# Decay attention and a soft mixture of experts on one core: the opening in another order with fewer filling products, part of the second layer in 256 columns, three more homes for expert weights

## The chip, the core and the metric

The kernel runs on one core of a Trainium2 chip. The time is device microseconds of the whole execution, and a kernel's time is the median of its runs. TensorE does the matrix products (PE; PEld is its weight load), VectorE (DVE), ScalarE (ACT) and GpSimd (POOL) do the rest, and SyncE (SP) issues every DMA of this kernel.

## What is computed

Two stages. The first is attention over 64 heads (8 batches of 8 heads), 576 tokens of width 64, with a causal mask and a decay that is a running sum of log f:

```python
log_f = np.log(np.clip(f, 0.0001, 1.0))
cum = np.cumsum(log_f, axis=-1)
decay = cum[:, :, :, None] - cum[:, :, None, :]
scores = np.where(causal, -1000000000.0, scale * q @ k.T + decay)
attn = np.exp(scores - np.max(scores, axis=-1, keepdims=True))
attn_out = (attn / (np.sum(attn, axis=-1, keepdims=True) + 1e-09)) @ v
```

The second takes its output as x (4608 tokens, width 512) through 32 slots of 8 experts, four slots each; softmax over all tokens on the way in (d), over slots on the way out (c):

```python
logits = x @ phi
slot_input = d.T @ x
for e in range(E):
    slot_out[e] = np.maximum(slot_input[e] @ w1[e], 0.0) @ w2[e]
out = c @ slot_out
```

Everything is float32. The weights w1 and w2 are 32 MB, the output 9.4 MB.

## The kernel before

**Attention.** The 64 heads are worked as 32 pairs, head i = 2g or 2g+1. Every product of 32-bit numbers q and k is made of rounded parts (WA for k, YA for q, rounded by ACT in `round_k` and `round_q`) and remainders (WB, YB; the remainders are subtracted on POOL by `low_k` and `low_q`, the rounded halves are copied beside them by a DMA, `dup_k` and `dup_q`). For a head PE makes scores with queries on the partitions (`s1`, L224), DVE takes their row maxima (`tops`, L240 and L238), PE turns the maxima (`mturn`, L250), ACT copies them (`mrows`, L259) and a DMA puts them as one more row into YA; then PE makes the scores again with keys on the partitions and the maxima already inside (`s2`, L277 and L278), ACT takes the exponential into PTS (`expo`, L284), POOL blanks what lies above the diagonal (`causal`, L292 for three blocks and L295 for the last two), and PE multiplies by V (`s3`, L312, 25 products a head), after which DVE divides (`norm`). A head's maxima are made one pair ahead of its `s2`. Scores of `s1` go to three PSUM tiles in rotation, those of `s2` to the three tiles of `ring`.

**Opening.** The first heads are written out by hand, call by call, ahead of the loop: `first(i, n)` is a quarter of `s1` and `tops` of head i, `both(i, n)` a quarter of `s2` and `expo`, `warm(n, cs)` n products whose result nobody reads (L495, "filling products"). Pair 0 gets its maxima by two transposes a head (`first_rows`, L573 and L576). Each engine runs its own instructions in the order in which the calls stand, and so does SP's DMA queue.

**The loop** over pairs g = 1 to 31 interleaves `s2` of pair g with `s1` of the pair after, turns pair g-1 of x (`px`, L339, copied by `xcopy`), and takes along the first steps of the mixture for a finished batch b (logits, a running maximum and sum, the slot inputs in `dispatch`, token weights in `combine`).

**Expert weights** are 64 quarters of 512 KB, used in the order `ORDER`. 27 have tiles of their own and are loaded in the loop; the others get a home as something else is finished with (`wstream`): buffers of q and k, of PTS, V and x, pools that open where the attention's tiles close, and, from the 45th on, the tiles of quarters that are used up.

**After the loop** the last batch's logits, sum and slot inputs run as one chain with other work between (`dispatch(b - 1, ...)`, `cols`). Then come the experts: `mlp1` (L910) makes four products of 256 columns for each quarter, each into another 32 partitions; `mlp2` (L948) makes for experts 0 to 3 two products of 512 columns a quarter, the first quarter of a half step into partitions 0 to 31 and 32 to 63, the second into the other 64, and for experts 4 to 7 four of 256. The output products (`blocks`, L1021) begin between the last of them; ACT and DVE copy them and SP writes them out.

## Time and profile before

| | us |
|---|---|
| median of three runs | 393.11 (392.79 to 394.31) |
| the profiled execution | 394.05 |
| its span, first to last instruction | 392.4 |
| PE, DVE, ACT, POOL busy | 372.9, 280.7, 260.1, 252.6 |
| mean granted clock of PE | 0.987 |

The span is 1.65 us shorter than the profiled execution's own time. Busy times are sums over a whole span that has four stages with different limits: opening (to 27 us), loop (to 324), the chain and the experts (to 362), output (to the end).

### The profile page before, as it was taken

Reading aid. Unit: us, or ns where it says so; the run is one execution under the profiler, and the core shown is the slowest. Engines: PE = TensorE matmul, PEld = TensorE weight load, DVE = VectorE, ACT = ScalarE, POOL = GpSimd, SP = SyncE. Lnnn points to the kernel's source line nnn. Section 1 sums busy time; section 2 is a strip of 40 time slices with the busy share of each in tenths; the row PEclk is TensorE's granted clock in tenths of the full one; section 3 lists DMA queues with packets and bytes.
Section 4 is the critical chain, followed back from the end, with each engine's and each line's share of the span. In section 5 each row is a group of like instructions: output and inputs, shape, how many; then the busy total and the mean of one; then the engine's idle time right before and its main releaser. Section 6 shows DMA issues by size and latency. Waiting matters only on the chain.

```text
span 392.4 us, 15020 instructions
## 1 busy us (share of the span) xinstructions
PE 372.9 (95%) x5827; PEld 330.1 (84%) x5827; DVE 280.7 (72%) x1074; ACT 260.1 (66%) x664; POOL 252.6 (64%) x349
## 2 busy tenths in 40 slices
PE   7999999999999999999999999999999999999860
PEld 7889999999999999999999999999899986545630
DVE  7878887878787878787879787878687535441761
ACT  8859786868686778677877686868686652021650
POOL 4797887878787878787878787878687831100000
PEclk9999999999999999999999999999999999999995
DMA  6865768677867777768777778778775879999798
GB/s 205 212 160 162 217 167 273 194 217 206 251 192 211 218 225 211 214 186 241 210 214 207 217 218 260 212 211 252 225 210 155 256 282 319 408 408 358 258 383 327
DMA packets 34343, 93.71 MB, mean 239 GB/s; under 512 B 4266, under 2 KB 8288, under 8 KB 34272
## 3 DMA queue, kind: packets, MB, share of 16 engines
q1 hardware_dynamic: 34272, 92.75, 76.3%
q8 instruction: 46, 0.75, 0.8%
q14 instruction: 25, 0.20, 0.2%
HBM read 63.93 MB, written 9.73 MB: 188 GB/s over the span
## 4 chain that ended last, share of the span: by engine, by line
PE 88%; DMA 4%; DVE 3%; ACT 2%; issue 1%; SPq 0%; ACTq 0%; DVEq 0%
PE pv L312 25%; PE ring L277 14%; PE s L224 13%; PE ring L278 13%; PE pv L339 5%; PE pv L948 4%; PE more L910 4%; PE lg L375 3%; DMA out<-RAW 2%; PE ds L459 2%; PE ring L495 1%; DMA YA<-mr 1%; PE pv L250 1%; DMA PTS<-in_f 1%; ACT PTS L284 1%
## 5 line engine op out<-in xcount | busy, mean ns | idle before, releaser
L284 ACT ACTIVATE PTS<-ring 128x320 f32<-128x320 f32 (+2 forms) x256 | 119.8, 513 | 65.2 <-PE ring L278 36.2
L277 PE MATMUL ring<-YA,WA 67*128 67x320 f32 (+9 forms) x384 | 121.9, 330 | 0.1
L240 DVE CUSTOM_DVE_ANT_0 s<-s,mask 128x320 f32<-128x320 f32 (+3 forms) x256 | 109.1, 442 | 5.4 <-PE s L224 0.9
L278 PE MATMUL ring<-YB,WB 128*128 128x320 f32 (+4 forms) x384 | 110.7, 296 | 0.0
L312 PE MATMUL pv<-V,PTS 128*64 128x65 f32 x3200 | 104.5, 223 | 1.1 <-ACT mr L259 0.7
L312 PEld LDWEIGHTS pv<-V,PTS 128*64 128x64 f32 x3200 | 99.7, 137 | 4.0 <-issue 1.8
L224 PE MATMUL s<-WA,YA 66*128 66x288 f32 (+9 forms) x384 | 98.5, 312 | 0.5 <-ACT YA L182 0.2
L203 POOL TENSOR_TENSOR WB<-RAW,WB 64x576 fp32r<-64x576 f32 x64 | 90.3, 1411 | 11.6 <-DMA WB<-WA 5.6
L208 POOL TENSOR_TENSOR YB<-RAW,YA 64x576 fp32r<-64x576 f32 x64 | 89.5, 1416 | 2.5
L277 PEld LDWEIGHTS ring<-YA,WA 67*128 67x128 f32 (+3 forms) x384 | 69.7, 183 | 5.8 <-issue 2.1
L278 PEld LDWEIGHTS ring<-YB,WB 128*128 128x128 f32 (+1 forms) x384 | 69.9, 182 | 0.0
L224 PEld LDWEIGHTS s<-WA,YA 66*128 66x128 f32 (+1 forms) x384 | 62.9, 190 | 7.0 <-ACT PTS L284 1.3
L295 POOL TENSOR_SCALAR_AFFINE_SELECT PTS<-PTS 128x128 f32<-128x128 f32 (+1 forms) x128 | 31.5, 268 | 25.6 <-ACT PTS L284 23.8
L240 DVE DVE_READ_ACCUMULATOR2_ANT MT<- 128x1 f32 x310 | 44.0, 142 | 0.0
L292 POOL TENSOR_SCALAR_AFFINE_SELECT PTS<-PTS 128x384 f32<-128x384 f32 x64 | 33.4, 522 | 15.1 <-ACT PTS L284 11.1
L339 PE MATMUL pv<-cs,X 128*128 128x128 f32 x155 | 42.0, 276 | 0.2 <-DVE lg L817 0.2
L240 DVE CUSTOM_DVE_ANT_0 s<-s,mask,MT 128x288 f32<-128x288 f32 x62 | 32.6, 526 | 11.4 <-PE s L224 2.4
L177 ACT CAST WA<-RAW 64x576 fp32r<-64x576 f32 x64 | 40.1, 669 | 0.8
L182 ACT CAST YA<-RAW 64x576 fp32r<-64x576 f32 x63 | 39.5, 669 | 0.4
L327 DVE TENSOR_SCALAR rl<-pv 128x5 f32<-128x5 f32 x64 | 10.5, 164 | 36.6 <-PE pv L312 36.0
L332 DVE TENSOR_TENSOR X<-pv,rl 128x320 f32<-128x320 f32 (+1 forms) x65 | 31.5, 486 | 2.4 <-DVE rl L328 0.3
L363 ACT COPY XT<-pv 128x128 f32<-128x128 f32 (+1 forms) x124 | 28.5, 290 | 0.0
(212 smaller groups left out, 373.1 us busy)
## 6 DMA issues: line engine op xcount, KB each, us to landing
w<-in_w SPq DMA_DIRECT2D x47, 512.0 KB
RAW<-in_qk SPq DMA_DIRECT2D x31, 576.0 KB
V<-in_v SPq DMA_DIRECT2D x32, 325.0 KB
...
```

What stands on the lines that cost most here:

```text
L177: nc.scalar.copy(WA[g % 3][0:64, S * h : S * h + S], RAW[g % 3][64:128, h])
L182: nc.scalar.copy(YA[g % 3][0:64, h, 64:640], RAW[g % 3][0:64, h])
L203: nc.gpsimd.tensor_tensor(t[0:64], RAW[g % 3][64:128, h], t[64:128].bitcast(F32), op=ALU.subtract)
L208: nc.gpsimd.tensor_tensor(YB[g % 2][64:128, h], RAW[g % 3][0:64, h], YA[g % 3][0:64, h, 64:640].bitcast(F32), op=ALU.subtract)
L224: nc.tensor.matmul(t[:, o : o + w], ya[0:m, h, 128 * blk : 128 * blk + 128], wa[0:m, j0 : j0 + w], start=True, stop=True)
L240: nc.vector.tensor_tensor_reduce(out=t[:, o : o + w], in0=t[:, o : o + w], in1=mask[:, m0 : m0 + w], scale=1.0, scalar=top if n == 3 else ...
L277: nc.tensor.matmul(o, wa[0:m, j0 : j0 + n], ya[0:m, h, 64 + i0 : 64 + i0 + w], start=True, stop=False)
L278: nc.tensor.matmul(o, wb[:, j0 : j0 + n], yb[:, h, i0 : i0 + w], start=False, stop=True)
L284: nc.scalar.activation(PT[i % 2][:, SEG_O[bank] : SEG_O[bank] + at], t[:, 0:at], AF.Exp, scale=0.125)
L292: nc.gpsimd.affine_select(d3, d3, pattern=[[0, 3], [1, 128]], compare_op=ALU.is_ge, fill=0.0, base=0, channel_multiplier=-1)
L312: nc.tensor.matmul(o[64 * u : 64 * u + 64, t, :], PT[i % 2][:, at : at + 64], V[:, g % 2, c, 65 * h : 65 * h + 65], start=(c == 0), stop=( ...
L339: nc.tensor.transpose(pm[:, 0:128], x[:, t, 128 * (p % 2) : 128 * (p % 2) + 128], ident)
```

## The change

1. *Opening.* RAW1's load moves behind the first `dup_k`; the second `dup_k`, the second `dup_q` and V's first load come earlier in SP's queue, the constant rows of tiles 2 and pair 2's load later. `fill` lies in X2, so that V's load need not wait for it. Of the filling products behind the first eleven, 15 become 9. `causal(0)` is cut in two, `low_k(2)` and `low_q(2)` stand earlier, `low_k(3)` and `low_q(3)` before `causal(1)`. `both(1, 2)`, `first(3, 2)` and `first(3, 3)` stand before `s3(0)`, `first(4, 1)` before `s3(1)`.
2. *Loop.* One quarter's load a pair for g = 2 to 28, in place of g = 4 to 28 with two at 22 and 26. In the last pair `px(30, 0)` stands after a block of `s2`; in the last two `mturn` and `mrows` stand before an `expo`. In pair 31 half of the last batch's logits stand between `s3(62)` and `s3(63)`.
3. *Homes.* XT's four tiles are one tile XTS, which gives two homes, and a tile w36 stands beside cT, which is shorter by 512 columns (`last` is longer). 47 quarters then have a first home and 17 reuse one; before it was 44 and 20.
4. *Second layer.* For experts 0 to 3 the products of `mlp2` are cut into two of 256 columns, but for the first half step of expert 0 and the last of expert 3.

```diff
-    load_qk(1)
-    fill = V.rearrange("p a t c -> p (a t c)")[:, 0:1280].bitcast(F32R)
+    fill = X[2].rearrange("p t c -> p (t c)").bitcast(F32R)
...
     round_k(0, 0)
+    dup_k(0, 0, 1)
+    load_qk(1)
     round_q(0, 0)
-    dup_k(0, 0, 1)
     dup_q(0, 0, 1)
     round_k(0, 1)
+    dup_k(0, 1, 2)
+    constant_rows(1)
...
-    warm(3 * WARM[1], cs)
+    warm(1, cs)
+    first(1, 3)
+    warm(1, cs)
     round_q(1, 0)
-    dup_k(1, 0, 1)
     dup_q(1, 0, 1)
+    constant_rows(2)
     both(0, 0)
-    first(1, 3)
     both(0, 1)
     first(2, 0)
     both(0, 2)
     nc.vector.tensor_copy(YA[1][0:64, 1, 64:640], RAW[1][0:64, 1])
-    warm(2, cs)
+    low_k(2)
+    causal(0, 0)
+    low_q(2)
     next(r1)
...
-    causal(0)
-    low_k(2)
-    low_q(2)
+    low_k(3)
+    low_q(3)
     both(1, 0)
     first(3, 0)
     both(1, 1)
-    warm(2, cs)
+    warm(1, cs)
...
     first(3, 1)
+    both(1, 2)
+    first(3, 2)
+    first(3, 3)
     round_k(2)
     s3(0)
-    both(1, 2)
-    first(3, 2)
-    round_q(2)
+    round_q(2, 0)
     both(1, 3)
-    first(3, 3)
     norm(0)
-    low_k(3)
     causal(1)
-    low_q(3)
-    first(4, 0)
-    warm(2, cs)
     mturn(1, 1, 2)
     mrows(1, 1, 2)
+    first(4, 0)
+    first(4, 1)
+    round_q(2, 1)
...
+        if g == NG - 1:
+            px(g - 1, 0)
...
-        expo(h1, 2)
+        if g < NG - 2:
+            expo(h1, 2)
         mturn(g + 1)
         mrows(g + 1)
+        if g >= NG - 2:
+            expo(h1, 2)
...
         if g == 31:
-            wstream(PTS[:, 0:QW])
+            logits(B - 1, 0, 1)
+            wstream(XTS[:, 0:QW], PTS[:, 0:QW])
...
-    wstream(X[0], X[1])
+    wstream(XTS[:, QW + 256 : 2 * QW + 256], X[0], X[1])
...
+                step = m if start or stop else 256
+                for c in range(0, m, step):
+                    nc.tensor.matmul(
+                        to[32 * (fc % 4) : 32 * (fc % 4) + 32, c : c + step],
+                        HT[e][:, fc // 2, fc % 2, :],
+                        w[:, m * n + c : m * n + c + step],
```

SP's queue behind the load of cs, before (WB<-WA is `dup_k`, YB<-YA `dup_q`, WA1<-PTS and cumd the decay rows, V_106 as a source is `fill`):

```order
L168 DMA RAW1_96<-in_qk 128x1152
L193 DMA WB0_92<-WA0_90 64x576
L197 DMA YB0_91<-YA0_89 64x576
L545 DMA WA1_86<-V_106 1x16x72
L546 DMA YA1_85<-V_106 2x1280
L193 DMA WB0_92<-WA0_90 64x576
L550 DMA WA1_86<-PTS_98 1x2x576 x2
L551 DMA cumd_74<-PTS_98 64x1152
L545 DMA WA2_94<-V_106 1x16x72
```

And now, from the same place:

```order
L191 DMA WB0_92<-WA0_90 64x576
L166 DMA RAW1_96<-in_qk 128x1152
L195 DMA YB0_91<-YA0_89 64x576
L191 DMA WB0_92<-WA0_90 64x576
L537 DMA WA1_86<-X2_101 1x16x72
L538 DMA YA1_85<-X2_101 2x1280
L553 DMA WA1_86<-PTS_98 1x2x576 x2
L195 DMA YB0_91<-YA0_89 64x576
L170 DMA V_103<-in_v 128x650
L560 DMA cumd_74<-PTS_98 64x1152
L191 DMA WB1_88<-WA1_86 64x576
```

Pair 0's first `dup_k` now has no load of 576 KB ahead of it, and pair 1's first `dup_k` has moved up from behind pair 2's load.

POOL in the opening, before, from the first `low_k` of pair 1's heads back to `causal(0)` (WB is `low_k`, YB `low_q`; PTS_98 with three blocks and with 128 and 64 columns is `causal`):

```order
L292 AFFINE_SELECT PTS_98<-PTS_98 128x3x128
L295 AFFINE_SELECT PTS_98<-PTS_98 128x128
L295 AFFINE_SELECT PTS_98<-PTS_98 128x64
L203 TENSOR_TENSOR WB1_88<-RAW1_96,WB1_88 64x576
L208 TENSOR_TENSOR YB1_87<-RAW1_96,YA1_85 64x576
L203 TENSOR_TENSOR WB1_88<-RAW1_96,WB1_88 64x576
L292 AFFINE_SELECT PTS_98<-PTS_98 128x3x128
L295 AFFINE_SELECT PTS_98<-PTS_98 128x128
L295 AFFINE_SELECT PTS_98<-PTS_98 128x64
L208 TENSOR_TENSOR YB1_87<-RAW1_96,YA1_85 64x576
```

And now:

```order
L201 TENSOR_TENSOR WB1_88<-RAW1_96,WB1_88 64x576
L291 AFFINE_SELECT PTS_98<-PTS_98 128x3x128
L206 TENSOR_TENSOR YB1_87<-RAW1_96,YA1_85 64x576
L294 AFFINE_SELECT PTS_98<-PTS_98 128x128
L294 AFFINE_SELECT PTS_98<-PTS_98 128x64
L201 TENSOR_TENSOR WB1_88<-RAW1_96,WB1_88 64x576
L206 TENSOR_TENSOR YB1_87<-RAW1_96,YA1_85 64x576
L291 AFFINE_SELECT PTS_98<-PTS_98 128x3x128
L294 AFFINE_SELECT PTS_98<-PTS_98 128x128
L294 AFFINE_SELECT PTS_98<-PTS_98 128x64
```

Both subtractions of head 3 now stand ahead of `causal(1)`, where one stood behind it.

PE around `s3(0)` (pv0, x25), before, from the filling products ahead of the turning of head 2's maxima:

```order
L495 MATMUL ring1_155<-cs_68 128x192 x2
L250 MATMUL pv0_152<-cs_68,MT1_114 5x128
L224 MATMUL s3_1_353<-WA1_86,YA1_85 128x288
L312 MATMUL pv0_152<-V_106,PTS_98 64x65 x25
L277 MATMUL ring1_155<-YA0_89,WA0_90 128x320
L278 MATMUL ring1_155<-YB0_91,WB0_92 128x320
L224 MATMUL s3_2_386<-WA1_86,YA1_85 128x288
```

And now:

```order
L494 MATMUL ring1_151<-cs_68 128x192
L248 MATMUL pv0_148<-cs_68,MT1_110 5x128
L222 MATMUL s3_1_347<-WA1_86,YA1_85 128x288
L275 MATMUL ring1_151<-YA0_89,WA0_90 128x320
L276 MATMUL ring1_151<-YB0_91,WB0_92 128x320
L222 MATMUL s3_2_353<-WA1_86,YA1_85 128x288
L222 MATMUL s3_3_356<-WA1_86,YA1_85 128x448
L222 MATMUL s3_3_356<-WA1_86,YA1_85 128x64
L311 MATMUL pv0_148<-V_103,PTS_98 64x65 x25
```

Three quarters of work that DVE and ACT wait for have moved ahead of the 25 products.

## Rows read from the trace of the kernel before

**Rows 1.** The page: the span, busy times, and PE's busy tenths in 40 slices.

```profile
span 392.4 us, 15020 instructions
PE 372.9 (95%) x5827; PEld 330.1 (84%) x5827; DVE 280.7 (72%) x1074; ACT 260.1 (66%) x664; POOL 252.6 (64%) x349
PE   7999999999999999999999999999999999999860
```

**Rows 2.** The page: the chain that ended last, shares of the span by engine.

```profile
PE 88%; DMA 4%; DVE 3%; ACT 2%; issue 1%; SPq 0%; ACTq 0%; DVEq 0%
```

**Rows 3.** PE in order of time in the opening: start, us, line, tiles, records, and the idle time before with what ended it.

```profile
14.98 0.81 PE L495 MATMUL ring<-cs 128*128 128x192 f32 x4
15.63 0.71 PE L573 MATMUL ring<-cs,LG 128*2 128x128 f32 x5
...
19.67 1.73 PE L312 MATMUL pv<-V,PTS 128*64 128x65 f32 x50 [0.21 <-ACT mr L259]
...
24.79 0.92 PE L312 MATMUL pv<-V,PTS 128*64 128x65 f32 x24 [0.25 <-ACT mr L259]
25.64 0.63 PE L224 MATMUL s<-WA,YA 66*128 66x288 f32 x3
26.20 1.03 PE L312 MATMUL pv<-V,PTS 128*64 128x65 f32 x26
27.16 0.47 PE L277 MATMUL ring<-YA,WA 67*128 67x448 f32 x1
```

**Rows 4.** POOL in order of time in the opening, columns as in rows 3.

```profile
10.33 1.40 POOL L203 TENSOR_TENSOR WB<-RAW,WB 64x576 fp32r<-64x576 f32 x1 [5.57 <-DMA WB<-WA]
...
18.25 0.49 POOL L295 TENSOR_SCALAR_AFFINE_SELECT PTS<-PTS 128x128 f32<-128x128 f32 x2 [0.96 <-ACT PTS L284]
19.63 1.41 POOL L203 TENSOR_TENSOR WB<-RAW,WB 64x576 fp32r<-64x576 f32 x1 [0.89 <-PE s L224]
21.10 1.42 POOL L208 TENSOR_TENSOR YB<-RAW,YA 64x576 fp32r<-64x576 f32 x1
...
24.07 0.52 POOL L292 TENSOR_SCALAR_AFFINE_SELECT PTS<-PTS 128x384 f32<-128x384 f32 x1
```

**Rows 5.** SP's queue in order of time: the issues of RAW1's load and of the first `dup_k`.

```profile
3.49 0.44 SPq L168 DMA_DIRECT2D RAW<-in_qk  x1
5.82 0.52 SPq L193 DMA_DIRECT2D WB<-WA  x1
```

**Rows 6.** The chain that ended last in order of time (start, us, what): the kernel's first load.

```profile
0.81 2.75 DMA PTS<-in_f
```

**Rows 7.** DVE in order of time in the opening, columns as in rows 3: the first maximum after `s3(0)`.

```profile
22.06 0.53 DVE L240 CUSTOM_DVE_ANT_0 s<-s,mask,MT 128x288 f32<-128x288 f32 x1 [2.09 <-PE s L224]
```

**Rows 8.** ACT in order of time, columns as in rows 3: the copy of head 3's maxima, and two exponentials of pair 30.

```profile
24.48 0.26 ACT L259 CAST mr<-pv 5x128 fp32r<-5x128 f32 x1 [0.35 <-ACT PTS L284]
...
311.63 0.81 ACT L284 ACTIVATE PTS<-ring 128x320 f32<-128x320 f32 x2
```

**Rows 9.** PE in order of time at the end of the loop, columns as in rows 3.

```profile
312.57 3.25 PE L312 MATMUL pv<-V,PTS 128*64 128x65 f32 x100 [0.25 <-ACT mr L259]
...
316.92 0.30 PE L339 MATMUL pv<-cs,X 128*128 128x128 f32 x1 [0.18 <-DVE lg L817]
...
323.49 1.18 PE L375 MATMUL lg<-XT,phis 128*32 128x128 f32 x24
324.61 0.77 PE L339 MATMUL ring<-cs,X 128*128 128x128 f32 x5
```

**Rows 10.** DVE in order of time behind `s3(63)`, the last head's division.

```profile
323.60 0.17 DVE L327 TENSOR_SCALAR rl<-pv 128x5 f32<-128x5 f32 x1 [0.33 <-PE pv L312]
...
324.02 0.56 DVE L332 TENSOR_TENSOR X<-pv,rl 128x128 f32<-128x128 f32 x2
```

**Rows 11.** Busy time by stretches: PE, PEld, DVE, ACT and POOL busy (instructions), granted clock, DMA share, GB/s.

```profile
322.00:324.00 2.00, 2.00 (x69) 1.93 (x69) 1.52 (x7) 0.03 (x1) 0.00 (x0) 1.00 0.46 96
328.00:330.00 2.00, 1.55 (x24) 1.07 (x27) 1.24 (x5) 1.54 (x6) 0.10 (x1) 1.00 0.99 295
332.00:362.00 30.00, 29.64 (x441) 15.01 (x445) 10.59 (x35) 4.86 (x14) 1.47 (x5) 1.00 1.01 403
374.00:391.00 17.00, 5.14 (x19) 2.65 (x18) 6.49 (x13) 4.87 (x9) 0.00 (x0) 0.73 1.02 385
```

**Rows 12.** PE in order of time among the experts' products, columns as in rows 3.

```profile
336.06 8.41 PE L910 MATMUL more<-w,EX 128*32 128x256 f32 x152
344.29 0.61 PE L910 MATMUL more<-RAW,EX 128*32 128x256 f32 x8
...
350.62 1.04 PE L948 MATMUL pv<-PTS,X 128*32 128x512 f32 x8
351.48 1.04 PE L948 MATMUL pv<-X,X 128*32 128x512 f32 x8
...
362.88 0.28 PE L1021 MATMUL more<-SO,cT 128*128 128x256 f32 x1
363.09 0.64 PE L948 MATMUL pv<-w,w 128*32 128x256 f32 x8
...
364.11 0.28 PE L1021 MATMUL ring<-SO,cT 128*128 128x256 f32 x1
364.37 0.64 PE L948 MATMUL pv<-w,w 128*32 128x256 f32 x8
```

More of the change, by code (lines that the diff above doesn't have):

```diff
@@ L104, in attn_softmoe @@
     X = [per.tile([P, NBLK, 256], F32, name=f"X{i}") for i in range(3)]
-    XT = [per.tile([P, S], F32, name=f"XT{i}") for i in range(NPAIR)]
+    XTS = per.tile([P, NPAIR * S], F32, name="XTS")
+    XT = [XTS[:, S * i : S * i + S] for i in range(NPAIR)]
     V = per.tile([P, 2, NBLK, 130], F32, name="V")
@@ L284, in expo, with causal @@
             nc.scalar.activation(PT[i % 2][:, SEG_O[bank] : SEG_O[bank] + at], t[:, 0:at], AF.Exp, scale=0.125)
-    def causal(i):
+    def causal(i, *parts):
         if not head(i):
@@ L290, in causal @@
         pt = PT[i % 2]
-        d3 = pt[:, 0:960].rearrange("p (a b) -> p a b", b=320)[:, :, 0:128]
-        nc.gpsimd.affine_select(d3, d3, pattern=[[0, 3], [1, 128]], compare_op=ALU.is_ge, fill=0.0, base=0, channel_multiplier=-1)
-        for o, w in ((pt_col(3, 384), 128), (pt_col(4, 512), 64)):
+        if 0 in parts or not parts:
+            d3 = pt[:, 0:960].rearrange("p (a b) -> p a b", b=320)[:, :, 0:128]
+            nc.gpsimd.affine_select(d3, d3, pattern=[[0, 3], [1, 128]], compare_op=ALU.is_ge, fill=0.0, base=0, channel_multiplier=-1)
+        for o, w in ((pt_col(3, 384), 128), (pt_col(4, 512), 64)) if 1 in parts or not parts else ():
             dd = pt[:, o : o + w]
@@ L526, in attn_softmoe @@
     nc.gpsimd.memset(EX[:, 192:256], 0.0)
+    for m in (1, 2):
+        nc.gpsimd.memset(YA[m][0:64, :, 0:64].bitcast(F32), 0.0)
+    nc.gpsimd.memset(fin[0:1, 4:5], -1.0)
     nc.vector.tensor_scalar(fx, fx, 1e-4, 1.0, op0=ALU.max, op1=ALU.min)
@@ L543, in attn_softmoe @@
     nc.vector.tensor_tensor(fp[lane, S:], fz, fp[lane, 0:S].bitcast(F32), op=ALU.subtract)
-    for m in (1, 2):
-        nc.sync.dma_start(WA[m][66:67].bitcast(F32), fill[0:1, 0 : 2 * S].bitcast(F32))
-        nc.sync.dma_start(YA[m][64:66].rearrange("c h s -> c (h s)").bitcast(F32), fill[32:34].bitcast(F32))
-        if m == 1:
-            dup_k(0, 1, 2)
-            for c in range(2):
-                nc.sync.dma_start(WA[1][64 + c : 65 + c].bitcast(F32), fp[65:98:32, S * c : S * c + S].bitcast(F32))
-            nc.sync.dma_start(cumd.rearrange("b a c s -> (b a) (c s)"), fp[lane].bitcast(F32))
+    for c in range(2):
+        nc.sync.dma_start(WA[1][64 + c : 65 + c].bitcast(F32), fp[65:98:32, S * c : S * c + S].bitcast(F32))
     for h in range(2):
@@ L562, in attn_softmoe @@
         low_q(h)
-    for m in (1, 2):
-        nc.gpsimd.memset(YA[m][0:64, :, 0:64].bitcast(F32), 0.0)
-    nc.gpsimd.memset(one, -1.0)
     round_k(1, 0)
+    dup_k(1, 0, 1)
+    load_qk(2)
     def first_rows(h):
@@ L614, in attn_softmoe @@
     expo(0, 3)
+    causal(0, 1)
     dup_q(1, 1, 2)
     dup_k(1, 1, 2)
-    load_cum(2)
+    load_v(1)
     load_qk(3)
@@ L677, in split @@
             nc.vector.tensor_tensor(lo, two, hi.bitcast(F32), op=ALU.subtract)
[L679 removed]
+    CUT = (9 * P, 13 * P)
     def weights_of(at, n):
         h, at = divmod(at, B // 2 * S)
[L684 removed]
+        o = at - CUT[h]
+        return last[h][:, o : o + n] if o >= 0 else cT[:, CUT[0] * h + at : CUT[0] * h + at + n]
     def cols(b, bank):
@@ L698, in cols @@
             yield
-    resident = iter(range(NRES))
     for g in range(1, NG):
@@ L711, in attn_softmoe @@
             load_v(g + 1)
-            for _ in range(TWICE.get(g, 1)):
-                wload(next(resident))
+        if 2 <= g < NRES + 2:
+            wload(g - 2)
         if w == 1:
@@ L837, in attn_softmoe @@
             wstream(RAW[29 % 3])
-    logits(B - 1, 0, 1, 2)
+    logits(B - 1, 2)
     wstream(V, PTS[:, QW : 2 * QW], PTS[:, 2 * QW : 3 * QW])
@@ L848, in attn_softmoe @@
     mx = turn()
-    nc.tensor.matmul(mx[0:1, 128:160], one[:, 0:1], row, start=True, stop=True)
+    nc.tensor.matmul(mx[0:1, 128:160], fin[0:1, 4:5], row, start=True, stop=True)
     dispatch(b - 1, 0, 1)
@@ L988, in attn_softmoe @@
             SO = sp.tile([P, DM], F32R, name="SO")
-            last = [sp.tile([P, 5 * P], F32R, name=f"cT{n}") for n in range(2)]
+            last = [sp.tile([P, B // 2 * S - CUT[n]], F32R, name=f"cT{n}") for n in range(2)]
         if (e, k) == (3, 6):
```

27 lines of the change are left out of this document (13 added, 14 removed).

## The prediction

> **What bounds the kernel now.** I read the page first: PE is busy for 372.9 of 392.4 us and at nine tenths or more in all slices but the first and the last three [rows 1], and 88% of the chain that ended last is PE's [rows 2]. So a microsecond that PE is spared, or an idle one that goes, is a microsecond of the kernel, wherever nothing else is late by as much; and a filling product counts like any other where PE would otherwise have work ready, and for nothing where PE would stand. The question in every place is which. For that I read the engines in order of time in the opening and at the loop's end [rows 3 to 10], then the stretches of the tail [rows 11] and the experts' products [rows 12]. The loop between has no idle PE to win: a shift at its start arrives at its end. Behind 374 us the DMA engines are full with output (share 1.02 [rows 11]) while PE has stopped; the bytes are the same, so that stage too only moves with the stage ahead of it.
>
> The sum is made against the profiled execution (394.05 us, 0.94 above the median of 393.11), and its result is taken off the median.
>
> **The opening.** Two filling products are four records and take 15.63 - 14.98 = 0.65 us [rows 3], so one takes 0.325 and the six that go 1.95 us: no more than this can come from leaving them out, and it comes only where the next product is ready.
>
> I follow the new order from the point where it parts from the old, with durations of the rows. Up to the transposes of head 1's maxima three products go; what they hid was ACT's and DVE's work on heads 0 and 1, of which `first(1, 3)` is now asked for sooner, and PE reaches the transposes at about 15.0 against 15.63, ahead by 0.6. From there it is bound by `tops` of head 2 and by ACT's exponentials, and stays 0.5 ahead. Then comes the main move. Before, DVE stood for 2.09 us over `s3(0)` [rows 7], because the scores of head 3 were made behind it. Now `both(1, 2)`, `first(3, 2)` and `first(3, 3)`, about 0.8 us of PE, stand ahead; `s3(0)` starts where it did (19.7) and ends at 21.4, as before, but behind it there is only `both(1, 3)` (0.5) and the turning of head 3's maxima, which DVE has ready by 21.5. ACT's exponential (0.6) and copy of the maxima (0.26 [rows 8]) then let `s3(1)` begin at about 22.9, against 24.79 [rows 3]: 1.9 us sooner. The three products of pair 2 that now stand in between are hidden in ACT's time.
>
> What is late next is POOL. `s3(1)` needs blocks 3 and 4 of `causal(1)` from its eighth product on, and both subtractions of head 3 now stand ahead of that. The queue in front of it: `dup_k(0, 0)` was issued at 5.82 behind RAW1's load [rows 5] and POOL had it at 10.33 [rows 4], 4.5 us later; the first load of the kernel, with nothing ahead, is there 2.75 us after its issue [rows 6]. With RAW1 behind it POOL can start at 5.8 + 2.75 = 8.6, and four subtractions of 1.45 end at 14.4 (before: 16.2). Pair 1's first `dup_k` is issued at 12.3, when ACT has rounded k, and is there between 15.1 and 16.8. Then follow a subtraction (1.41), three blocks (0.52), a subtraction (1.42), two blocks (0.49) [rows 4], with gaps to 19.1 or 20.8. The second `dup_k` of pair 1 is issued at 17.25 and is there between 20.0 and 21.75; two subtractions and `causal(1)` behind it take 2.9 + 1.05, to 23.95 or 25.7. So `s3(1)` stands 0.75 us in its eighth and ninth product (to 23.95), has 0.2 us left of its first part, and 0.56 and 0.96 follow (25.64 to 27.16 [rows 3]): the loop begins at 25.65 in place of 27.16. I take **-1.5**. The bounds: no stall at all (`dup_k` as quick as need be), -1.9; both `dup_k` as slow as the one behind RAW1, 25.7 + 1.7 = 27.4, +0.2. I take the value at 2.75 us because the reordered queue has moved V's load and the decay rows into the idle DMA time ahead of 12 us, and pair 2's load is through by 17.
>
> The other edits of the opening cost nothing: three memsets of POOL fall into its 5.57 us of waiting [rows 4]; the constant rows and cumd's rows of pair 2, now later in SP's queue, are needed at 22 and issued by 16; RAW1 is needed at 11.6, where ACT's table load ends, and is issued at 6.3. Two quarters' loads in pairs 2 and 3 in place of doubled ones later lie in DMA time that is free.
>
> **The loop's end.** In pair 30 PE waits 0.25 us for ACT's copy of the maxima [rows 9], behind two exponentials of 0.81 together [rows 8]. With the copy ahead of the second it is ready 0.35 sooner, and the wait goes: -0.3 with the issue beside it. In pair 31 `px(30, 0)` waits for a division; the block of `s2` that now stands ahead (0.3 us of PE) fills the gap from 316.6 to 316.92: **-0.3** (both are bounded by 0 and -0.4).
>
> Half of the last logits move ahead of `s3(63)`. They are 16 of the 24 records of 1.18 us [rows 9], 0.79 us, which used to hide the last division (323.60 to 324.58 [rows 10]): before, PE came out of the logits at 324.61 just as the division was done. Now `s3(63)` and its division come 0.79 later and only 0.39 us of logits cover a division of 1.0: the transposes start about 0.55 later. The work is the same; its cover is gone. **+0.55** (between 0, if POOL held `s3(63)` up anyway, and +0.8).
>
> **Homes.** Between 322 and 324 the DMA engines stood half idle (0.46), and from 332 to 362 they were full (1.01) [rows 11]: three more quarters fetched early end the weights' stream by about 3 us sooner. But PE, 29.64 busy of these 30 us, does not wait for them until the last two quarters, which start 0.21 and 0.26 us behind the product before them [rows 12], against 0.11 where products follow each other. **-0.2** (0 to -0.4). The early loads hide; they do not shorten.
>
> **Products of 256 columns.** Eight records of 512 columns take 351.48 - 350.62 = 0.86 us, and 152 of 256 take 344.29 - 336.06 = 8.23 [rows 12], 0.108 and 0.054 each, and both go to four different groups of 32 output partitions. Cut in two, six half steps of eight records become sixteen: 0.86 and 0.87 us. If the four groups stay equally full that is **+0.05**, which I take as the nearest row. But a group's two halves now stand next to each other in the program, and no row shows such a sequence. Its other end: if only two groups work side by side, sixteen records take 1.73 and the six half steps 6 x 0.87 = 5.2 us more. Below nothing there is no room, since a column costs the same in both.
>
> A rule of the Trainium skill bears on this (TensorE: Matmul & The Clock Gate, Part 3: Packing small matmuls): matmuls start and end in program order, without reordering, and only other groups overlap. By that rule the sum would carry the 5.2. The rows speak against its strict form: each product leaves two records, the second for the same group, and still eight records of 256 columns pass in the time of two alone; so something is drawn past already, how far they don't show.
>
> **Sum.** -1.5 - 0.3 - 0.3 + 0.55 - 0.2 + 0.05 = -1.7: 392.35 for an execution like the profiled one, **391.4** off the median.
>
> **Rivals.**
> *POOL takes the fillers' place.* `s3(1)` waits for `causal(1)` behind two slow `dup_k`: the opening gives +0.2 in place of -1.5, and the whole 393.1. For it: POOL had a subtraction less ahead of `causal(1)` before, and stood for nothing from 19.63 on. Against: its chain begins 1.7 us sooner.
> *Everything comes free.* No stall, no loss at the logits' move: -1.9 - 0.6 + 0.3 - 0.4 = -2.6, 390.5. For it: the load behind RAW1 was the slowest of its kind.
> *The halves of a group get in each other's way* in `mlp2`, at 350 us. In full, +5.2: 396.6, slower. It decides the sign from 1.7 / 6 = 0.28 us per half step and passes the bound of slower at 0.6. In part (a third of the groups' overlap lost, 0.2 a half step) +1.2: 392.6. For it: nothing here shows two neighbours in one group among four. Against: the rows on pairs of records just told.
> *The clock.* Fewer filling products leave PE idle; but where PE was busy for 1.55 of 2 us the granted clock stayed at 1.00 [rows 11], and no stretch of the new opening is emptier. I leave it in the last 2%.
>
> **Chances.** Forecast 0.52, with its own range 390.9 to 392.1; POOL's rival 0.16; everything free 0.13; halves in part 0.12, in full 0.06; the rest 0.01. From 390.4 to 393.5 holds the first four but for their edges. A measurement of this kernel tells 0.5% from no change, so faster is below 391.1: the free case and 0.16 of the forecast, 0.29. Slower is above 395.1: 0.07. Within: 0.64.
>
> **What would show it.** In the changed profile: POOL's first subtraction near 8.6; DVE without its gap of 2 us; `s3(1)` beginning near 22.9 with a wait for POOL in it; the loop's first `s2` near 25.65; no wait for ACT's copy in pair 30; a gap of half a microsecond on PE behind the last logits, ahead of L339's successor; w's loads ending about 3 us ahead of the first output; records of 256 columns in `mlp2` at 0.054 us. The prediction is wrong if the loop begins later than 26.6 or `mlp2` of experts 0 to 3 takes over 8 us.

## The result: slower, by the clock of TensorE

| | before | after |
|---|---|---|
| median of 15 runs each, us | 393.35 (392.42 to 395.06) | 397.92 (392.84 to 414.82) |
| ratio | | 1.006 (1.0035 to 1.0084) |
| the profiled execution, us | 394.05 | 398.77 |
| its span, us | 392.4 | 397.0 |
| mean granted clock of PE | 0.987 | 0.971 |

The prediction was 391.4. The ratio leaves out every run that is over 1.5% above its kernel's fastest, and here that leaves out six executions of which the text below speaks: the median of all 15 is 1.2% above. The time goes with the clock: two executions at a mean clock of 0.989 took 392.84 and 392.91 us, two at 0.982 and 0.985 took 394.3 and 394.6, ten at 0.965 to 0.976 took 397.2 to 401.3. One at 0.845 took 414.8, which no profile explains.

The page of the changed kernel shows it: PE is less busy than before in the third slice alone (7 tenths in place of 9), and PEclk has a hole in the third and fourth, where that of before had none.

```profile
span 397.0 us, 15097 instructions
PE   7979999999999999999999999999999999999860
PEclk9975999999999999999999999999999999999995
```

Busy time by stretches of the opening (PE, PEld, DVE, ACT, POOL busy, granted clock, DMA share, GB/s):

```profile
20.00:22.00 2.00, 1.35 (x36) 1.31 (x36) 0.70 (x4) 1.88 (x3) 0.72 (x3) 1.00 0.89 265
22.00:24.00 2.00, 1.33 (x12) 1.08 (x10) 1.60 (x6) 0.60 (x1) 1.67 (x2) 1.00 0.76 256
24.00:26.00 2.00, 0.46 (x8) 0.46 (x10) 0.55 (x3) 0.77 (x2) 1.93 (x4) 0.87 0.05 14
26.00:28.00 2.00, 2.00 (x25) 1.66 (x21) 0.31 (x1) 0.06 (x1) 1.92 (x3) 0.50 0.16 35
...
36.00:40.00 4.00, 4.00 (x31) 3.81 (x31) 2.42 (x8) 1.94 (x8) 1.61 (x2) 0.61 0.01 2
```

The emptiest of these stretches, in the profile of before:

```profile
24.00:26.00 2.00, 1.75 (x30) 1.39 (x29) 1.86 (x7) 0.38 (x2) 1.85 (x4) 1.00 0.02 3
```

PE stood for 2.9 of the 6 us from 20 to 26, then the granted clock fell to 0.50 (1.2 in place of 2.4 GHz) in the 26th, and came back in the stretch that ends at 40; PE was busy all the time between. What it stood for, in PE's order of time (answers to [rows 3]):

```profile
19.28 0.68 PE L311 MATMUL pv<-V,PTS 128*64 128x65 f32 x14
20.65 1.46 PE L311 MATMUL pv<-V,PTS 128*64 128x65 f32 x36 [0.69 <-POOL PTS L294]
...
25.54 1.57 PE L311 MATMUL pv<-V,PTS 128*64 128x65 f32 x24 [2.21 <-ACT mr L257]
...
29.71 0.74 PE L275 MATMUL ring<-YA,WA 67*128 67x448 f32 x1
```

`s3(0)` stands 0.69 for POOL's last blocks, `s3(1)` 2.21 for ACT's copy of the maxima, and the loop begins at 29.71 against 27.16. The chain that ended last says what ACT waited for (start, us, what):

```profile
14.51 5.94 DMA YB<-YA
...
20.46 0.02 SPq L260
...
20.51 4.62 DMA YA<-mr
...
25.23 0.26 ACT mr L257
```

The copy of head 3's maxima goes into the tile `mr`, of which there is one, and so waits until the DMA of head 2's maxima has read it. That DMA was issued at 20.51, behind the loads of V and of pair 3 in SP's queue (before, V's stood behind it), and landed 4.62 us later; its issue itself waited for a `dup_q` of 14.51, eight transfers earlier in the queue. POOL would not have let `s3(1)` through either (columns as in [rows 4], whose rows these answer to):

```profile
8.29 1.60 POOL L201 TENSOR_TENSOR WB<-RAW,WB 64x576 fp32r<-64x576 f32 x1 [3.21 <-DMA WB<-WA]
...
16.73 1.41 POOL L201 TENSOR_TENSOR WB<-RAW,WB 64x576 fp32r<-64x576 f32 x1 [1.70 <-ACT WA L175]
...
22.25 1.41 POOL L201 TENSOR_TENSOR WB<-RAW,WB 64x576 fp32r<-64x576 f32 x1 [1.47 <-DMA WB<-WA]
23.73 1.39 POOL L206 TENSOR_TENSOR YB<-RAW,YA 64x576 fp32r<-64x576 f32 x1
...
25.67 0.49 POOL L294 TENSOR_SCALAR_AFFINE_SELECT PTS<-PTS 128x128 f32<-128x128 f32 x2
```

Its first subtraction comes as early as forecast; pair 1's two, which wait for `dup_k` issued at 12.74 and 17.41, start at 16.73 and 22.25, and `causal(1)` ends at 26.2. (The row at 16.73 names ACT's rounding, which was done at 12.3; what came last was the `dup_k`.) Pair 2's load, which the forecast had through by 17, is what ACT waits for until 19.96:

```profile
19.96 1.24 ACT L175 CAST WA<-RAW 64x576 fp32r<-64x576 f32 x2 [0.84 <-DMA RAW<-in_qk]
```

Where the 4.6 us between the two spans arise, from PE's order of time in both:

| start of | before | after | later by |
|---|---|---|---|
| first `s2` of the loop | 27.16 | 29.71 | 2.55 |
| `s3(10)` | 70.33 | 76.77 | 6.44 |
| `s2` of pair 31 | 315.75 | 320.88 | 5.13 |
| transposes behind the last division | 324.61 | 330.13 | 5.52 |
| second layer | 348.03 | 353.59 | 5.56 |
| end of the second layer | 365.01 | 370.63 | 5.62 |
| end of the span | 392.41 | 397.03 | 4.62 |

Of the 1.3 us that it wins back in the loop, 0.6 is a hitch of the profiled execution of before: its pair 26 took 9.50 us, that of the changed kernel 8.86. 0.3 is pair 30, and what remains are small differences of other pairs, none over 0.2. The end of the loop, columns as in [rows 9]:

```profile
317.70 3.25 PE L311 MATMUL pv<-V,PTS 128*64 128x65 f32 x100
320.88 0.47 PE L275 MATMUL ring<-YA,WA 67*128 67x448 f32 x1
...
322.05 0.52 PE L338 MATMUL pv<-cs,X 128*128 128x128 f32 x3
...
330.13 0.81 PE L338 MATMUL ring<-cs,X 128*128 128x128 f32 x5 [0.35 <-DVE X L331]
```

`s3(60)` no longer waits for ACT and `px(30, 0)` no longer for DVE; the transposes now wait 0.35 for the last division. The second layer's products of 256 columns run at the pace of [rows 12]: from the row at 354.49 to that at 359.65 there are 96 records in 5.16 us, 0.054 each.

```profile
354.49 0.42 PE L959 MATMUL pv<-RAW,X 128*32 128x256 f32 x2
354.69 0.41 PE L959 MATMUL pv<-p,X 128*32 128x256 f32 x2
...
359.65 0.62 PE L959 MATMUL pv<-X 128*32 128x512 f32 x2
```

The last 1.0 is won behind the second layer, where nothing of the change seemed to lie.

### The profile page after: what moved, and what is told of

Its sections match the earlier page's. It is cut to its first block, busy times and chain, and to the rows that moved or that the text cites. A ratio compares the mean times of both kernels' runs of the same rounds, so it can differ in the third digit from the quotient of the medians.

```text
span 397.0 us, 15097 instructions
## 1 busy us (share of the span) xinstructions
PE 375.6 (95%) x5863; PEld 336.8 (85%) x5863; DVE 280.8 (71%) x1074; ACT 260.9 (66%) x664; POOL 253.1 (64%) x349
## 4 chain that ended last, share of the span: by engine, by line
PE 88%; DMA 6%; DVE 2%; ACT 1%; issue 1%; ACTq 0%; DVEq 0%; SPq 0%
PE pv L311 26%; PE ring L275 14%; PE ring L276 13%; PE s L222 13%; PE pv L338 5%; PE pv L959 4%; PE more L919 4%; PE lg L374 3%; DMA out<-RAW 3%; PE ds L458 2%; DMA YB<-YA 1%; DMA YA<-mr 1%; PE pv L248 1%; DMA PTS<-in_f 1%; PE ring L1036 1%
## 5 line engine op out<-in xcount | busy, mean ns | idle before, releaser
L275 PE MATMUL ring<-YA,WA 67*128 67x320 f32 (+9 forms) x384 | 123.4, 334 | 0.0
L276 PE MATMUL ring<-YB,WB 128*128 128x320 f32 (+4 forms) x384 | 112.1, 300 | 0.0
L311 PE MATMUL pv<-V,PTS 128*64 128x65 f32 x3200 | 106.3, 225 | 2.9 <-ACT mr L257 2.2
L311 PEld LDWEIGHTS pv<-V,PTS 128*64 128x64 f32 x3200 | 101.2, 139 | 6.0 <-ACT mr L257 2.4
L222 PE MATMUL s<-WA,YA 66*128 66x288 f32 (+9 forms) x384 | 100.2, 317 | 1.0 <-ACT WA L555 0.7
L275 PEld LDWEIGHTS ring<-YA,WA 67*128 67x128 f32 (+3 forms) x384 | 71.1, 186 | 5.6 <-issue 2.1
L276 PEld LDWEIGHTS ring<-YB,WB 128*128 128x128 f32 (+1 forms) x384 | 71.4, 186 | 0.0
L222 PEld LDWEIGHTS s<-WA,YA 66*128 66x128 f32 (+1 forms) x384 | 64.5, 195 | 7.4 <-ACT PTS L282 1.4
L326 DVE TENSOR_SCALAR rl<-pv 128x5 f32<-128x5 f32 x64 | 10.5, 164 | 39.1 <-PE pv L311 38.5
L236 DVE TENSOR_REDUCE MT<-s 128x1 f32<-128x288 f32 x62 | 27.9, 450 | 1.7 <-PE s L222 1.7
```

Source lines behind the costliest of these rows:

```text
L222: nc.tensor.matmul(t[:, o : o + w], ya[0:m, h, 128 * blk : 128 * blk + 128], wa[0:m, j0 : j0 + w], start=True, stop=True)
L275: nc.tensor.matmul(o, wa[0:m, j0 : j0 + n], ya[0:m, h, 64 + i0 : 64 + i0 + w], start=True, stop=False)
L276: nc.tensor.matmul(o, wb[:, j0 : j0 + n], yb[:, h, i0 : i0 + w], start=False, stop=True)
L311: nc.tensor.matmul(o[64 * u : 64 * u + 64, t, :], PT[i % 2][:, at : at + 64], V[:, g % 2, c, 65 * h : 65 * h + 65], start=(c == 0), stop=( ...
```

## The experiments

Theory A: the whole loss is made in the opening; ACT's copy and POOL keep PE standing, and PE's standing costs the clock. Rival B: the loss lies behind the opening. Rival C: in the opening it is one of the two waits alone. All runs; each ratio is to the kernel before in the run's own series, formed as that of the result:

| run | median, us (range, runs) | ratio to before |
|---|---|---|
| open_alone | 399.65 (395.74 to 401.35, 4) | 1.0144 (1.0086 to 1.0202) |
| rest_alone | 392.15 (391.98 to 392.50, 7) | 0.9972 (0.9960 to 0.9983) |
| hold | 393.86 (393.23 to 399.93, 10) | 1.0014 (1.0002 to 1.0027) |
| both_ends | 392.28 (391.93 to 392.85, 10) | 0.9978 (0.9968 to 0.9989) |
| mr_two | 394.66 (393.10 to 400.78, 10) | 1.0039 (1.0004 to 1.0073) |
| pool_order | 393.11 (392.07 to 400.17, 10) | 0.9992 (0.9977 to 1.0007) |
| homes_back | 392.58 (392.02 to 398.07, 10) | 0.9983 (0.9972 to 0.9994) |
| logits_back | 391.60 (391.57 to 391.95, 4) | 0.9959 (0.9944 to 0.9974) |
| joined | 391.18 (390.51 to 392.24, 7) | 0.9948 (0.9930 to 0.9966) |
| joined2 | 391.87 (391.01 to 399.80, 10) | 0.9970 (0.9944 to 0.9997) |
| queue | 396.84 (391.83 to 400.54, 10) | 1.0039 (1.0003 to 1.0075) |
| cut_back | 392.22 (391.98 to 393.44, 9; a tenth took 1995) | 0.9977 (0.9963 to 0.9990) |
| halves_back | 393.40 (392.88 to 394.04, 10) | 1.0005 (0.9992 to 1.0018) |
| count_only | 392.48 (392.19 to 393.33, 9) | 0.9978 (0.9968 to 0.9988) |
| before_count | 392.84 (392.34 to 393.87, 10) | 0.9986 (0.9974 to 0.9998) |

**open_alone and rest_alone: the opening, and all but the opening.** The texts of the two openings are exchanged, between `lane = slice(64, 128)` and the end of `s3(1)`.

> The kernel before with the opening of the changed kernel alone. Theory A (the whole loss is made in the opening: ACT's copy of head 3's maxima waits for the transfer of head 2's, PE stands for 2.2 us, and its granted clock falls to 0.50 for some 12 us): about 398, as the changed kernel's median of 397.9, with the mean clock of most executions between 0.965 and 0.976, and now and then one near 393.5 at 0.989. Rival B (the loss is made behind the opening, by the products of 256 columns, the logits' move or the homes): 392 to 393.5, at 0.987.

> The changed kernel with the opening of before. Theory A: as before or a little faster, 392.0 to 393.3 (behind the opening the trace of the changed kernel shows -0.3 at the pairs' end, +0.7 at the last division, +0.03 in the second layer and -1.0 in the output), clock 0.987. Rival B: 396 to 398.

Both came out as theory A has it. The opening alone makes the kernel slower by as much as the whole change, at clocks of 0.968 to 0.985, and its profile has the clock at 0.50 from 25 to 39 us too. There `s3(1)` stands shorter for ACT than in the changed kernel's profile, and then for POOL:

```profile
24.56 0.68 PE L313 MATMUL pv<-V,PTS 128*64 128x65 f32 x14 [1.27 <-ACT mr L259]
25.73 0.91 PE L313 MATMUL pv<-V,PTS 128*64 128x65 f32 x10 [0.50 <-POOL PTS L296]
```

The rest alone makes the kernel faster by 1.1 us at 0.986 to 0.990. Rival B falls.

**hold: the same stall, with PE kept busy in it.**

```diff
     dup_q(2)
     dup_k(2)
+    warm(7, cs)
     s3(1, None, 12)
```

> The changed kernel with seven more filling products directly ahead of s3(1), 7 x 0.325 = 2.3 us, the length of the stall; nothing that s3(1) waits for comes sooner by them. Theory A: PE is busy through the stall, the clock stays at 1.00, s3(1) starts where it did (25.5 to 25.7), the loop's first s2 at 28.0 to 28.2 in place of 29.71, and the time is 392.5 to 394 at a mean clock near 0.988. If the fall of the clock came from elsewhere: 397 to 398.5, with the fall still there.

Busy time by stretches of its profile, columns as above, and its PE rows:

```profile
22.00:24.00 2.00, 2.00 (x21) 1.93 (x18) 1.49 (x6) 0.60 (x1) 1.41 (x2) 1.00 0.78 284
24.00:26.00 2.00, 2.00 (x23) 1.77 (x22) 0.66 (x3) 0.83 (x2) 1.93 (x3) 1.00 0.01 2
26.00:28.00 2.00, 2.00 (x41) 1.69 (x39) 0.69 (x3) 0.00 (x0) 1.92 (x4) 1.00 0.64 123
```

```profile
25.65 1.29 PE L311 MATMUL pv<-V,PTS 128*64 128x65 f32 x24
...
28.39 0.47 PE L275 MATMUL ring<-YA,WA 67*128 67x448 f32 x1
```

`s3(1)` starts as late as in the changed kernel (25.65 and 25.54), and still the loop begins 1.3 us sooner and `s3(10)` at 71.53 in place of 76.77, because the clock holds. So seven products that compute nothing are worth 5.2 us, and this is what the fall of the clock costs. It held in nine of ten executions; the tenth ran at 0.973 and took 399.93. What is left of the opening's loss at full clock is 71.53 - 70.33 = 1.2 us in this profile.

**both_ends, mr_two, pool_order: the two waits, both and each alone.**

```diff
+        if (g, h0) == (1, 0):
+            mr = X[1].rearrange("p t c -> p (t c)")[0 : 2 * NBLK, 0:P].bitcast(F32R)
+        else:
             mr = small.tile([2 * NBLK, P], F32R, name=f"mr{g}_{h0}", tag="mr", bufs=1)
...
     low_k(3)
-    low_q(3)
...
     causal(1)
+    low_q(3)
     mturn(1, 1, 2)
```

mr_two has the first piece alone, pool_order the other.

> The changed kernel with two things mended in the opening: head 2's maxima get a place of their own, so that the copy of head 3's need not wait for their transfer, and POOL's low_q(3) stands behind causal(1) again. Theory A: s3(1) starts at 23.6 (exponential done at 23.47, copy 0.26) and stands at its eighth product until about 24.6, the loop's first s2 near 26.4, clock 1.00 throughout, the time 391.2 to 392.2. Rival C (something else of the opening, as the late dup_k, holds s3(1) all the same): s3(1) passes its eighth product behind 25.7, the clock falls, 396 to 398.

> The changed kernel with a place of its own for head 2's maxima, and nothing else mended. If the copy's wait alone makes the stall: s3(1) starts at 23.6 and runs through, the loop's first s2 near 26.2, 391.5 to 392.8. If POOL holds it just as long (both subtractions of head 3 stand ahead of causal(1), which ended at 26.2 in the changed kernel): s3(1) starts at 23.6, stands about 2 us at its eighth product, the granted clock falls, first s2 at 28 or later, 395.5 to 398.

> The changed kernel with low_q(3) behind causal(1) again, and nothing else mended. If the copy's wait alone suffices for the stall: s3(1) starts between 24.5 and 25.5, when the transfer of head 2's maxima has landed, runs through, PE stands for 1.2 to 2.2 us ahead of it; first s2 at 27.2 to 28.1 where the clock holds, later where it falls; the executions scatter between 393 and 398 with clocks of 0.97 to 0.988. If POOL alone makes the stall: 391.5 to 392.8.

PE's rows: both_ends, mr_two and pool_order, in this order.

```profile
23.69 1.04 PE L314 MATMUL pv<-V,PTS 128*64 128x65 f32 x24 [0.32 <-ACT mr L260]
...
26.18 0.47 PE L278 MATMUL ring<-YA,WA 67*128 67x448 f32 x1
```

```profile
23.32 0.68 PE L314 MATMUL pv<-V,PTS 128*64 128x65 f32 x14 [0.32 <-ACT mr L260]
26.04 0.91 PE L314 MATMUL pv<-V,PTS 128*64 128x65 f32 x10 [2.04 <-POOL PTS L297]
```

```profile
24.42 0.92 PE L311 MATMUL pv<-V,PTS 128*64 128x65 f32 x24 [1.04 <-ACT mr L257]
...
26.80 0.47 PE L275 MATMUL ring<-YA,WA 67*128 67x448 f32 x1
```

Each mending alone leaves the other wait: with a place for the maxima `s3(1)` begins at 23.32 and stands 2.04 us for POOL a few products on; with POOL's order mended ACT's copy still waits for the transfer, and `s3(1)` stands 1.04. So there are two waits, one behind the other, and a trace shows only the one that ends last. They are not equal. With the maxima's place alone the clock still falls (in the profile to 0.50 for 3.4 us from 26.1; four of ten executions are at 0.982 or less), and the median of 394.66 lies between the two expectations. With POOL's order alone nine of ten keep theirs (0.985 to 0.989), the loop begins at 26.80, sooner than the 27.2 to 28.1 expected, and the time is that of before; what the transfer's wait still costs, 393.11 against 392.28, is not clear of the noise (the intervals overlap). So rival C is nearly right of POOL. The 2.21 us of the changed kernel's profile were a late transfer's: ACT's copy starts there at 25.23, and at 24.1 to 24.3 in the profiles of open_alone, hold and pool_order, which have the same queue.

With both mended the loop begins at 26.18, 1.0 us ahead of before, and no execution lost its clock (0.986 to 0.990). Its time, 392.28, is a little above what was expected, and no better than rest_alone's with the opening of before (392.15). A reason shows in another profile with the same opening (joined, below): there `s3(1)` stands for POOL again, and the loop begins at 27.87.

```profile
25.76 0.65 PE L314 MATMUL pv<-V,PTS 128*64 128x65 f32 x10 [1.37 <-POOL PTS L297]
...
27.87 0.47 PE L278 MATMUL ring<-YA,WA 67*128 67x448 f32 x1
```

POOL's first subtraction for head 3, in both_ends and then in joined:

```profile
21.78 1.41 POOL L201 TENSOR_TENSOR WB<-RAW,WB 64x576 fp32r<-64x576 f32 x1 [0.96 <-DMA WB<-WA]
```

```profile
23.48 1.40 POOL L201 TENSOR_TENSOR WB<-RAW,WB 64x576 fp32r<-64x576 f32 x1 [2.63 <-DMA WB<-WA]
```

So in these two profiles, the fastest execution of the one and the slowest of the other, this opening's start varies by 1.7 us, as much as the landing of the second `dup_k`; that of before, with its fillers, began between 27.16 and 27.48 in all eight profiles that have it.

**queue: why `dup_k` is late.** In the kernel joined, 620 KB are taken from ahead of pair 1's first `dup_k`:

```diff
     dup_q(0, 1, 2)
-    load_v(0)
-    nc.sync.dma_start(cumd.rearrange(...), fp[lane].bitcast(F32))
...
     dup_k(1, 0, 1)
+    load_v(0)
+    nc.sync.dma_start(cumd.rearrange(...), fp[lane].bitcast(F32))
     load_qk(2)
```

> The kernel with both mendings and the logits back (391.18), with V's first load and the rows of the running sum behind pair 1's first dup_k in SP's queue, where they stood ahead of it. If the 620 KB ahead of it make that dup_k late (issued at 12.74 and there at 16.5 in the changed kernel): it is issued at 12.3 to 12.7 and there by 15.3, POOL's first subtraction of pair 1 starts 1.0 to 1.5 sooner than 16.7, s3(0) loses its 0.6 to 0.7 of standing; time 390.6 to 391.2. If a transfer of its kind takes 4 us in this stretch whatever stands ahead: POOL's subtraction at 16.3 to 16.8 again, 391.0 to 391.7.

Its rows on POOL:

```profile
16.06 1.51 POOL L201 TENSOR_TENSOR WB<-RAW,WB 64x576 fp32r<-64x576 f32 x1
...
24.21 1.39 POOL L201 TENSOR_TENSOR WB<-RAW,WB 64x576 fp32r<-64x576 f32 x1 [3.98 <-DMA V<-in_v]
```

(The row names V's load, which signals by the same semaphore as the second `dup_k`, issued at 18.53 and there at 24.1.) The first expectation holds for what it was made for: the transfer issued at 12.74 is there by 15.1 (POOL takes it up when it is done with pair 0 at 16.06), and `s3(0)` runs through. But what follows now comes later: POOL has the second `dup_k` at 24.21, against 23.48 in joined and 22.25 in the changed kernel, `s3(1)` stands 1.84 for it, and the clock falls in most executions: 396.84, outside both expectations. With the DMA engines at a share of 0.93 to 1.10 from 12 to 16 us in the changed kernel, a transfer that is moved up moves another down.

**homes_back and logits_back: two parts of the rest undone, in rest_alone.** The first leaves out the calls of `wstream` for w36 and for the two homes in XTS; the second is

```diff
-            logits(B - 1, 0, 1)
-            wstream(XTS[:, 0:QW], PTS[:, 0:QW])
+            wstream(PTS[:, 0:QW])
...
-    logits(B - 1, 2)
-    wstream(V, PTS[:, QW : 2 * QW], PTS[:, 2 * QW : 3 * QW])
+    logits(B - 1, 0, 1, 2)
+    wstream(XTS[:, 0:QW], V, PTS[:, QW : 2 * QW], PTS[:, 2 * QW : 3 * QW])
```

> The changed kernel with the opening of before and without the three new homes (44 first homes and 20 reuses as before). By the prediction's term for the homes (-0.2) against the same kernel with the homes, 392.15: 392.3 to 392.5. By what the two traces show behind the second layer (26.0 us from its end to the end of the span with the homes, 27.4 in the kernel before): the last weights land while the first output is written, the stretch is 27.0 to 27.4 long again, and the time is 393.1 to 393.5.

> The changed kernel with the opening of before and with the last batch's logits behind s3(63) again (the home in XTS then comes after them). By the trace the move costs 0.75 on PE's path between s3(62) and the experts; if that reaches the end: 391.3 to 391.6 against 392.15 with the move. If the output stage is bound by its own DMAs, so that an earlier start of it gives nothing, as an opening that was 1 us shorter gave nothing: 391.9 to 392.3.

The homes are worth 0.4 us by the medians, but the intervals of the two ratios overlap, and cut_back, which lacks the homes too, took 392.22: a gain is not shown. The stretch behind the second layer stays 26.0 long without them: the second expectation was wrong. One execution of homes_back took 398.07 at a clock of 0.980, with the opening of before; no profile shows why. The logits' move costs 0.55 by the medians; the ranges of the two kernels do not overlap (391.95 and 391.98 are their ends), the intervals of the ratios do.

**halves_back, cut_back: what shortens the output.** One line of rest_alone, and the cut of the output weights in homes_back:

```diff
-                step = m if start or stop else 256
+                step = m
```

```diff
-    CUT = (9 * P, 13 * P)
+    CUT = (13 * P, 13 * P)
```

> The changed kernel with the opening of before and the second layer's products of experts 0 to 3 in 512 columns again. By the prediction's term (+0.05 for the cut, four groups that stay full): 392.0 to 392.3 against 392.15, the second layer 16.98 long in place of 17.03. By the rival (halves of one group stand in each other's way, 0.2 to 0.87 a half step): 391 down to 387.

> The changed kernel with the opening of before, without the three homes and with the output weights cut as before (26 columns of 128 in the first tile, 5 and 5 in the others). Behind the second layer the span took 27.4 and 27.2 us in the two profiles with the old cut and 26.0 to 26.4 in all with the new one. If the cut makes that: 27.2 to 27.4 again, and 393.3 to 393.8 against 392.58. If not: 26.0 to 26.4, 392.4 to 392.8.

The cut of the output weights does nothing. The products in 512 columns again cost 1.25 us, which no expectation had: the second layer itself is as long as before (16.93 against 17.03), but behind it the span takes 27.0 in place of 26.0. In SP's order of time the issues of the first outputs take about 0.4 us each (the last ten mostly 1.0 to 1.2, in every kernel), but for one, here of halves_back, and then of before:

```profile
371.47 1.03 SPq L1036 DMA_DIRECT2D out<-RAW  x1
```

```profile
370.42 1.91 SPq L1024 DMA_DIRECT2D out<-p  x1
```

In rest_alone no issue near it takes over 0.5. The view of the DMA queues from 370 to 373 us shows what came beside it in the profile of before (busy tenths and GB/s in 40 slices; q8 is a load of instructions, 16 KB):

```profile
DMA  9999999820599999899510000100101100000069
GB/s 369 369 410 396 382 341 587 273 69 0 218 328 328 369 396 355 314 396 382 164 28 0 0 0 0 14 0 14 14 0 14 14 0 27 14 27 27 27 246 410
...
q8 instruction: 1, 0.02, 3.0%
```

The same view of rest_alone has no q8 row, and the engines are never idle:

```profile
DMA  9998889999999999999999999998999999989999
...
q1 hardware_dynamic: 1067, 1.02, 103.3%
```

In rest_alone that load comes at 362.2, when DMA has stood (share 0.04 from 360 to 362) and the first output has just been issued. The cut of the second layer makes PE's program 48 records longer (5875 in place of 5827 on the page). That this is why the load comes sooner is what the next two runs try.

**count_only and before_count: the same count of instructions, in another place.** In halves_back, and in the kernel before:

```diff
+                step = 128 if e > 4 and k in (1, 2) else 256
+                for c in range(0, 256, step):
                     nc.tensor.matmul(
-                        PH[e][32 * j : 32 * j + 32, 0:256], ...
+                        PH[e][32 * j : 32 * j + 32, c : c + step], ...
```

> The changed kernel with the opening of before, the second layer in 512 columns again (393.4 in the last row), and in its place 24 products of the first layer (experts 5 to 7, k = 1 and 2) cut into two of 128 columns: PE's program gets the 48 instructions that the cut of the second layer gave it, ahead of the outputs, and nothing else changes. If the gain of 1.2 comes from where an instruction load of 16 KB falls (at 371.2, between the outputs, where SP's issue then took 1.03 in place of 0.40; with the cut at 362.2, where the DMA engines stand): the load falls near 362, no issue of SP between the 9th and the 18th output is over 0.5, and the time is 392.1 to 392.6 (first layer up to 0.3 longer). If the gain is the second layer's own: 393.3 to 393.9.

> The kernel before with the same 24 products of the first layer cut, and nothing of the change. By the instruction load (at 370.5, SP's issue 1.91 long): it falls near 362, and the time is 1.0 to 1.3 below the kernel before's 393.1: 391.8 to 392.3. If not: 393.1 to 393.6.

Both loads fell at 362.0 to 362.1, and no issue ahead of 373 us took over 0.64. count_only gives 392.48, ratio 0.9978 against 1.0005 for halves_back; before_count makes the kernel before faster by 0.14%, 0.5 us, with an edit that spares no work at all. That is less than the 1.0 to 1.3 expected. So the gain comes with the count of the records ahead of the outputs, and the load's place moves with it; that the load makes the loss, by holding up SP's issue, is argued from a coincidence in time. For it: the load lies among the outputs' writes in four profiles (before at 370.5, halves_back 371.2, open_alone 378.3, queue 371.2), and the issue beside it takes 1.03 to 1.91; in the 13 others it lies within 1 us of the first output's issue, and no issue there takes over 0.81. The stretch behind the second layer is 27.0 to 27.4 long in the first three, and 25.9 to 26.4 in the 13. Against: in queue it is 26.4, although the issue beside its load took 1.20; that load came 1.8 us behind the first output's issue, the other three 8 to 11. In which way it does so stays open.

**joined and joined2: the best of both.** joined is both_ends with the logits back as in logits_back; joined2 puts `low_q(2)` behind the whole of `causal(0)` as well.

> The changed kernel with both mendings of the opening and with the last logits behind s3(63) again. If the opening's 1.06 (first s2 at 26.18 against 27.24) and the logits' 0.75 both reach the end: 390.6 to 391.0, from 392.15 less 0.55 as measured for the logits and less 1.0. If the opening's gain varies from execution to execution with the transfers that its stalls hang on, as the mended opening alone (392.28) against the opening of before (392.15) says: 391.5 to 391.9.

> As the kernel of the last row, with low_q(2) behind the whole of causal(0) on POOL, so that s3(0) need not stand 0.7 us for its last blocks. The prediction's way of counting: s3(0) runs through from 19.3, ends at 21.0, s3(1) starts at 22.9 to 23.2, the loop's first s2 at 25.7 to 25.9, a clock that holds, and 0.3 to 0.4 less than the last row. If DVE and the pair's dup_k hold the next steps anyway: first s2 at 26.2 again, no change of time.

joined, at 391.18, is faster than both kernels, by 0.5% (interval 0.3 to 0.7%) against before, and its clock held in all seven executions. Its middle lies between the two expectations. joined2 is a miss: `s3(0)` runs through, but PE then stands 0.92 for ACT and 0.82 for POOL, the loop begins at 26.99 in its profile, and three of ten executions lost the clock (395.5 to 399.8).

## Why the prediction was wrong, point by point

*What bounds the kernel* was right as far as it went: a microsecond at the loop's start arrives at its end. That holds in the wrong direction too, and the argument took PE's own speed as given.

*The opening, -1.5.* It was +1.2 in the profile of hold, whose clock held, and +6.4 with the clock's fall. Three steps failed. First, "ACT's exponential (0.6) and copy of the maxima (0.26 [rows 8]) then let `s3(1)` begin at about 22.9": the durations were right, but the copy has a wait of its own, for the DMA that reads the single tile `mr`, and that DMA stands behind two loads in SP's queue, of which the new order had put V's ahead of it. The queue was followed for `dup_k` and not for the five rows of maxima. In before this wait was hidden because head 3's maxima were turned so late: the copy of 24.48 waits only for ACT itself [rows 8]. Second, "I take the value at 2.75 us because the reordered queue has moved V's load and the decay rows into the idle DMA time ahead of 12 us, and pair 2's load is through by 17": from issue to POOL's start pair 1's `dup_k` took 4.0 and 4.8 us, the second more than the upper bound of 4.5. Those bytes were then ahead of it in a queue that had no idle time left (share 0.93 to 1.10 from 12 to 16 us), and pair 2's load was through at 19.96. Its consequence was foreseen as the rival "POOL takes the fillers' place", and the runs bear out that POOL's order is the larger of the two waits. That rival's 393.1 is close to the 392.8 and 392.9 of the two executions with a steady clock, but in part by luck: its opening, +0.2, was too cheap, and the rest of the change won more than the sum has. Third, "I leave it in the last 2%": the clock. The row that it rested on, 1.55 of 2 us at clock 1.00, was taken as if it covered any stall, with "no stretch of the new opening is emptier"; the new opening had 1.33 and then 0.46 of 2 us. Its own [rows 11] have a stretch with 5.14 of 17 us, and there the clock is 0.73. Right were the start of POOL's chain (8.29, forecast 8.6), head 3's maxima ready before `s3(0)` ends (DVE is done with them at 20.7, forecast 21.5), and PE's lead at the second transposes (14.67 against 15.63: 0.96, forecast 0.6).

*Pair 30, -0.3*: 8.82 to 8.50 us. Right. *Pair 31, -0.3*: 7.75 to 7.44 us in the changed kernel's profile, but to 7.65 in rest_alone's, where the pair's first `s2` waits for the transfer of the maxima:

```profile
314.92 0.47 PE L275 MATMUL ring<-YA,WA 67*128 67x448 f32 x1 [0.20 <-DMA YA<-mr]
```

The wait that the edit removes is 0.18 in its own row [rows 9], not the 0.3 that was read from 316.6; the sum had no term for the new one.

*The logits, +0.55*: 0.35 of standing and 0.7 on PE's path; undoing it gave 0.55. Right.

*The homes, -0.2*: between nothing and 0.4. Not contradicted, and not shown.

*Products of 256 columns, +0.05*: right for the second layer, 17.03 against 16.93 to 16.98, and both rivals fell: two neighbours in one of four groups of partitions cost no more than 0.1. The strict order that the Trainium skill states (TensorE: Matmul & The Clock Gate, Part 3: Packing small matmuls) would, by the prediction's reading, have added 5.2; the trace does not agree with it for this sequence. In the program the eight records of the first quarter (p) stand ahead of those of the second (RAW), yet RAW's begin at 354.49 and p's go on at 354.69.

*The output* was put at nothing: "the bytes are the same, so that stage too only moves with the stage ahead of it". That was wrong: 24 more products ahead of it went with an output that is 0.5 to 1.3 us faster, and with a load of instructions that moved out of it.

Without its opening the change was forecast at -0.3 - 0.3 + 0.55 - 0.2 + 0.05 = -0.2 us. It measured -1.1; the output, which the forecast put at nothing, gave -1.25 by halves_back, so the gain is not that of the terms that were summed.
